# A one-step maximum over partitions, and another order of the first tile's statistics, weights and products in a fused LayerNorm, FFT and FFN kernel

## The chip, the cores and the metric

The kernel runs on one core of one Trainium2 chip. The metric is the device time of one execution in microseconds; lower is better. A run's time is a little longer than the span of its instructions in the profile.

## The reference

The kernel computes, for x of 8192 tokens by 448 features (f32), a layer norm, then two branches of it: a Fourier mixing branch (a transform over tokens and features, a small block-diagonal complex MLP with soft shrinkage on the spectrum, and back) and a GeGLU feed-forward branch. Their product is added to x.

```python
xn = _layernorm(x, axis=-1)
s = _A_ref(xn, A_w1, A_b1, A_w2, A_b2)
g = _silu(_B_ref(xn, B_w_gate, B_w_up, B_w_down))
return x + s * g
# _B_ref(x, w_gate, w_up, w_down) = (_gelu(x @ w_gate) * (x @ w_up)) @ w_down, F = 1792
```

The change touches neither the spectral branch's formulas nor the feed-forward's; it concerns how the first data and weights get ready.

## The kernel before, in words

The engines are TensorE (PE, with its weight loads as PEld), VectorE (DVE), ScalarE (ACT), GpSimd (POOL) and SyncE (SP), which issues the DMAs. Every operation is recorded through one helper, so almost every row of the profile has the same line (L180 before, L182 after); rows are told apart by the names of their tiles.

**Precision.** Products with f32 accuracy are made of f16 pieces: each operand is split into a high half (rounded to f16) and a low half (the remainder), and a product is the sum of high by high, high by low and low by high. Weights are first scaled by a power of two, which needs the largest magnitude of a weight block over all partitions and columns.

**Stages.** Tokens come in 16 chunks of 512 (four tiles of 128). Phase 1 normalises each chunk, makes the first step of the Fourier transform (`stage1`, tiles `m`, `ysb`, rows `bf<-xs,m`) and writes the pieces that the feed-forward needs to memory. The feed-forward (`ffn`) runs through the whole kernel: the first two chunks with 8 of the 14 weight tiles by plain products (`plain`, three terms), the others by a scheme with fewer products (`unit`, `product`) which needs combinations of the weights (`gu_comb`); the other 6 weight tiles follow in a second pass. Phase 2 does the spectral MLP, phase 3 the inverse transform (rows `bf<-u,mt`) and the final product; both are threaded between the feed-forward's matmuls on PE.

**The order of work.** A planner (`Pace`) runs while the kernel is built. Tasks are Python generators; each yields a time or an event, and the planner keeps a modelled time of each engine (`pace.free`), of each region of each tile, and of the last operation (`pace.last`). It records operations in the order of these modelled times; each engine then executes its operations in exactly that order. So a change of a cost in `Pace.cost` or of a due time (`T1`, `DT`, `END1`, `END2`, `END3`) reorders the programs of all engines. `Either` (`B`) sends an operation to DVE or POOL, whichever ends first by the model.

**The start.** `load_x` brings the first chunk's four tiles (in the order 0, 2, 1, 3), `gu_loads` the weight tiles `wst` of 704 KB each into four buffers. `begin` takes two tiles at a time (0 and 2, then 1 and 3): sums on DVE (`BN_STATS`, `BN_AGGR`), the power on POOL, a refinement on DVE (the root), the normalisation (`norm`, rows `x<-x,st`), and then per tile `token`: ACT casts to the high half `xs`, POOL or DVE subtracts for the low half, PE transposes both into a bank (`bf` or `bk<-ident,xs`), and a copy brings them to `xta`, tiles 0 and 2 by ACT, 1 and 3 by DVE. `gu_block` handles the weights of block b: DVE reduces the magnitudes over the columns (`fm<-wst`, then `fx<-fm`), `largest` takes the maximum over partitions, three small DVE steps make the scales (`fh`, `fc`, `fe`), and `gu_split` makes the high half on ACT and the low half on DVE or POOL (`wt`). For the first tile the halves are `ACTIVATE wt<-wst,fc` and `SCALAR_TENSOR_TENSOR wt<-wst,fc,wt`, each for up (4 slices) and gate (4 slices). `largest` works in two steps: an f32 matmul with the identity turns the columns of maxima into rows (`bf<-identf,fx`), DVE reduces along them (`mxr<-bf`), a second f32 matmul with the result repeated as weights brings it to all partitions (`bf<-identf,mxr`), and DVE copies it with a floor (`fx<-bf`).

`plain(0, 0)`, the first weight tile on the first chunk, works on two halves of 256 tokens; in each it goes through up and gate, and in each of these slice by slice: high by high, high by low, low by high. `down_weights(0)` loads the down-projection weights (`wo`, `xtb`, `cb<-in_down`), takes their maxima in eight DVE reductions (`dmx`) and splits them to `dw`; the down products (`bk<-dw,h`) come after both first chunks' `plain`.

Of the kernel before, what the change touches and what calls it, by code (L numbers as in the profile page):

```python
# [48 lines left out]
class Pace:  # L49
# [334 lines left out]
def afno_geglu_kernel(ctx, tc, x, gu, wd, mlp, b1, b2, c_m, c_mt, c_small, out):  # L384
# [32 lines left out]
    def part(bank_, *shape):  # L417
# [3 lines left out]
        return v.rearrange("p (a b) -> p a b", a=shape[1]) if len(shape) == 3 else v  # L421

    def pe():
        return pace.free.get("PE", 0.0) - 0.3
# [27 lines left out]

    def largest(dst, src, floor):

        w = src.shape[-1]
        b = yield from BF.get()
        T.matmul(b[0:w, 0:128], src, identf, start=True, stop=True)
        yield
# [86 lines left out]

    def norm(c, a):
        x4, st = EV["x4", c], EV["st", c]
        V.tensor_scalar(x4[:, a, :], x4[:, a, :], st[:, a, 6:7], st[:, a, 11:12],
                        op0=ALU.subtract, op1=ALU.mult)
# [103 lines left out]

    T1, DT = 84.0, 40.0

# [10 lines left out]
    def gu_block(b, to):  # L666

        f0, n = BLK[b]
        for i in range(n):
            yield ev("wl", f0 + i, 0)  # L670
            t = EV["wst", f0 + i, 0]
            V.tensor_reduce(fm[:, i, :, b], t[:, 0:8].rearrange("p (i k) f -> p i (k f)", i=2),
                            axis=AXIS.X, op=ALU.max, apply_absolute_value=True)
            yield
        mx = fx[:, :, b]
        if n == 2:
            V.tensor_tensor(mx, fm[:, 0, :, b], fm[:, 1, :, b], op=ALU.max)
        else:
            V.tensor_copy(mx, fm[:, 0, :, b])
        yield  # L680
# [6 lines left out]
        pow2(e, mxa)  # L687
        yield
        S.activation(fc[:, 4, b:b + 1], e[:, 1:2], AF.Copy, scale=2.0 ** -20)
        S.activation(fc[:, 5, b:b + 1], half[:, 1:2], AF.Copy, scale=2.0 ** (-25 - 2 * to))  # L690
        done("scales", b)
        for i in range(n):
# [4 lines left out]
            else:  # L697
                d, k = (yield from WO.get()), 2
            yield from gu_split(f, t, d, k)
            done("w", f)  # L700
            if to == 0:
# [20 lines left out]
    def gu_split(f, t, d, k):  # L722
# [443 lines left out]
    def plain(c, f):  # L1166

        yield ev("w", f)
        xT, h = EV["xT", c], EV["hT", c]
        g, u = (yield from BX.get()), (yield from BY.get())  # L1170
        w = wt[f]
        for q, tk in enumerate((slice(0, 256), slice(256, 512)) if (c, f) == (0, 0) else (slice(0, 512),)):
            if f == 0:
                for a in ((0, 2), (1, 3))[q] if c == 0 else range(CH):
                    yield ev("xp", c, a)
            for p, v in ((u, 0), (g, 4)):
                for t in range(3):
# [555 lines left out]

    END1, END2, END3 = T1 + NG * DT + 12.0, 1480.0, 1780.0

# [91 lines left out]
    def token(c, a, xs):  # L1827
# [31 lines left out]
    def begin():  # L1859
# [7 lines left out]

        def half(q):
            yield from stats(0, V, (q, q + 2))
            for a in (q, q + 2):  # L1870
                norm(0, a)
                tasks.append(pace.spawn(token(0, a, xss[a // 2]), pace.last))
                yield
# [8 lines left out]
        ST.put(EV["st", 0])  # L1882
        for q in range(2):
# [52 lines left out]
    def first():  # L1936
# [8 lines left out]
        tasks = []  # L1945
        yield 28.0
        done("phase", 1)
# [34 lines left out]
```

## Time and profile before

| | us |
|---|---|
| median of three runs | 1845.62 |
| lowest, highest | 1842.31, 1846.54 |
| the profiled execution | 1843.94 |
| its span, first to last instruction | 1842.2 |
| TensorE busy in the span | 1774.8 |
| VectorE, ScalarE, GpSimd busy | 1423.4, 1096.9, 582.9 |

In a timeline row stand the start, the duration, the engine, the line, the operation, `out<-in`, the shapes and a count (several like instructions are merged); in brackets the engine's idle time ahead of it and what ended that. The recorded duration of a PE row includes its latency, so the distance from one start to the next tells what it costs in a dense stretch. In a row of the stretches stand the length, and then for each engine the busy time and in parentheses the number of instructions. The mean granted TensorE clock of the profiled execution is 0.996.

### The profile page before, as it was taken

How to read it: one execution, taken by the hardware profiler on the slowest of the kernel's cores; microseconds unless marked ns; L12 is line 12 of the kernel's file. 1: busy time of each engine (PE TensorE's matmuls, PEld its weight loads, DVE VectorE, ACT ScalarE, POOL GpSimd, SP SyncE). 2: the span in 40 equal slices, each digit the busy share in tenths (PEclk: the TensorE clock that was granted, in tenths of full speed). 3: DMA queues.
4: the chain of work that ended last, by engine and by line, in shares of the span. 5: the costliest groups of instructions: out<-in, count | busy, mean ns of one | idle time of the engine just before them, and what ended most of it. 6: DMA issues, size and time to landing. Idle time of an engine off the chain costs nothing. (4 is left out here: it accounts for less than half of the span.)

```text
span 1842.2 us, 39141 instructions
## 1 busy us (share of the span) xinstructions
PE 1774.8 (96%) x15649; PEld 1423.5 (77%) x15649; DVE 1423.4 (77%) x2418; ACT 1096.9 (60%) x2105; POOL 582.9 (32%) x629
## 2 busy tenths in 40 slices
PE   6999999999999999999999999999999999999997
PEld 3447567666777777887877899989989898878886
DVE  7867788776866666656767788888888897888888
ACT  4746566655655555566766777677777774434443
POOL 3334444324523313100101233334432342333332
PEclk9999999999999999999999999999999999999999
DMA  7463665586564552132235544543344435999984
GB/s 263 140 168 113 195 193 177 164 233 186 147 165 115 150 155 82 44 92 74 64 114 166 147 104 117 117 104 88 98 103 117 112 97 156 327 297 319 289 311 148
DMA packets 345655, 287.79 MB, mean 156 GB/s; under 512 B 231840, under 2 KB 312736, under 8 KB 345472
## 3 DMA queue, kind: packets, MB, share of 16 engines
q1 hardware_dynamic: 345328, 285.26, 53.9%
q8 instruction: 122, 2.00, 0.4%
q14 instruction: 61, 0.50, 0.1%
q10 hardware_dynamic: 144, 0.03, 0.0%
HBM read 129.47 MB, written 106.61 MB: 128 GB/s over the span
## 5 line engine op out<-in xcount | busy, mean ns | idle before, releaser
L180 PEld LDWEIGHTS <-wt 128*128 128x128 f16 x9350 | 908.7, 98 | 191.6 <-issue 26.6
L180 PE MATMUL bk<-xta,wt 128*128 128x256 f16 (+1 forms) x5190 | 635.2, 276 | 9.2 <-DVE wt L180 4.6
L180 PE MATMUL bk<-xtb,wt 128*128 128x256 f16 x3120 | 382.2, 273 | 7.7 <-ACT v L180 7.7
L180 PE MATMUL bk<-dw,h 128*128 128x448 f16 (+1 forms) x2208 | 375.1, 321 | 9.0 <-DVE h L180 4.1
L180 PEld LDWEIGHTS <-h 128*128 128x128 f16 x2688 | 257.8, 98 | 140.8 <-DVE h L180 5.7
L180 ACT COPY v<-bk 128x512 f32<-128x512 f32 x208 | 121.7, 585 | 100.6 <-PE bk L180 99.3
L180 ACT COPY u<-bk 128x512 f32<-128x512 f32 x208 | 121.2, 585 | 70.9 <-PE bk L180 65.2
L180 POOL TENSOR_TENSOR wt<-wt 128x256 f32<-128x256 f32 x92 | 81.2, 883 | 185.9 <-DVE wt L180 174.4
L180 DVE TENSOR_TENSOR u<-bk,u 128x512 f32<-128x512 f32 x104 | 71.3, 686 | 86.4 <-PE bk L180 85.9
L180 POOL TENSOR_TENSOR zs<-t,zs 112x256 f16<-112x256 f32 (+2 forms) x41 | 35.5, 865 | 303.4 <-ACT zs L180 297.7
L180 ACT ACTIVATE u<-u,fc 128x512 f32<-128x512 f32 (+1 forms) x118 | 77.7, 669 | 62.0 <-DVE u L180 61.6
L180 PE MATMUL bk<-dw,wt 128*128 128x224 f16 (+1 forms) x864 | 103.1, 269 | 8.1 <-DVE pt L180 8.0
L180 POOL TENSOR_TENSOR v<-v,u 128x512 f32<-128x512 f32 x40 | 61.2, 1531 | 156.5 <-ACT v L180 152.5
L180 DVE SCALAR_TENSOR_TENSOR pt<-bk,fb,pt 128x448 f32<-128x448 f32 x112 | 74.7, 677 | 32.9 <-PE bk L180 32.0
L180 ACT CAST h<-wt 128x512 f16<-128x512 f32 (+1 forms) x128 | 68.6, 538 | 48.7 <-DVE wt L180 36.3
L180 ACT ACTIVATE th<-bk,fb 128x448 f32<-128x448 f32 x64 | 40.5, 633 | 85.4 <-PE bk L180 59.8
L180 PE MATMUL bf<-w2t,wn 112*128 112x112 f16 x1512 | 84.9, 213 | 0.0
L180 PEld LDWEIGHTS <-wn 112*128 112x128 f16 x1512 | 80.6, 98 | 2.4
L180 DVE TENSOR_TENSOR v<-bk,v 128x512 f32<-128x512 f32 x104 | 71.0, 683 | 12.9 <-PE bk L180 11.4
L180 POOL TENSOR_TENSOR h<-wt,h 128x512 f16<-128x512 f32 (+1 forms) x50 | 62.8, 1260 | 39.7 <-ACT h L180 37.8
L180 PEld LDWEIGHTS <-w1t 112*112 112x112 f16 x612 | 68.1, 130 | 7.5 <-issue 2.9
L180 DVE TENSOR_SCALAR x<-x,st 128x448 f32<-128x448 f32 x72 | 56.0, 790 | 22.3 <-POOL st L180 22.1
(197 smaller groups left out, 2934.4 us busy)
## 6 DMA issues: line engine op xcount, KB each, us to landing
wst<-in_gu SPq DMA_DIRECT2D x22, 704.0 KB, 5.4
xts<-sx SPq DMA_DIRECT2D x32, 480.0 KB, 2.9
x<-in_x SPq DMA_DIRECT2D x17, 896.0 KB, 5.9
t<-ysb SPq DMA_DIRECT2D x64, 224.0 KB, 3.4
prt<-th SPq DMA_DIRECT2D x64, 224.0 KB, 2.6
pt<-prt SPq DMA_DIRECT2D x64, 224.0 KB, 4.4
u<-t SPq DMA_DIRECT2D x32, 448.0 KB, 5.6
y<-t SPq DMA_DIRECT2D x30, 448.0 KB, 3.5
```

The source lines that it names most:

```text
L180: return self.pace.issue(self.name, kind, out, ins, lambda: fn(out, *args, **kw))
```

## The change

**`largest` in one step** for up to four columns: for each column one f32 matmul takes the column, repeated 128 times, as weights and the identity as moving data, so that each partition of the bank gets all 128 values; one DVE reduction over 128 columns per value then gives the maximum on all partitions. The floor moves into the step ahead (`fx<-fm`, now a scalar_tensor_tensor or tensor_scalar). This holds for all eight weight blocks and for the four-column maximum of the spectral weights; the down weights' eight and six columns keep the two steps.

**The first tokens.** The sums of both pairs of tiles come first; then the first pair's root and normalisations, then the first weight tile's maximum over columns, then the second pair's root, then the maximum over partitions and the scales, then the second pair's normalisations. The identity's f32 copy is made by ACT instead of DVE. Which engine copies a transposed bank is chosen by the planner's free times, no longer by the tile's number.

**The first weight tile.** Its other maxima's tasks start only once it is split. `plain(0, 0)` starts when the high halves are there, and in each half of the tokens takes first high by high for up and gate, then the inputs' low part, then the low weights. The small factors on ACT come after the split.

**Down weights** are started after weight tile 4 instead of tile 1.

**Due times** and costs: `T1` 84 to 78, `END2` 1480 to 1472, `END3` 1780 to 1772, the second chunk's start 28 to 26; the modelled cost of a DVE copy from f16 is smaller.

In the order of DVE's program before, from the first normalisation on (`x_102` are the first chunk's tokens, `st` their statistics, `wst` the raw weights, `fm` and `fx` their maxima):

```order
L180 TENSOR_SCALAR x_102<-x_102,st 128x448
L180 TENSOR_REDUCE fm<-wst 128x2
L180 TENSOR_SCALAR x_102<-x_102,st 128x448
L180 COPY fx<-fm 128x2
L180 BN_STATS st<-x_102 128x6
L180 BN_AGGR st<-st 128x2
```

And after, from the end of the second pair's sums to the same place:

```order
L182 TENSOR_SCALAR st<-st 128x2
L182 TENSOR_TENSOR st<-st 128x2 x2
L182 TENSOR_SCALAR st<-st 128x2
L182 TENSOR_TENSOR st<-st 128x2
L182 TENSOR_SCALAR x_102<-x_102,st 128x448 x2
L182 TENSOR_REDUCE fm<-wst 128x2
L182 TENSOR_SCALAR fx<-fm 128x2
```

The second pair's `BN_STATS` stood behind the weights' maximum and now stand ahead of the first pair's root; both normalisations stand together ahead of the maximum.

Further on in DVE's program, before, around the low half of the first weight tile (`wt0_82`; `wst_130` and `wst_138` are raw weights of later tiles):

```order
L180 TENSOR_SCALAR x4_102<-x4_102,st_122 128x448
L180 TENSOR_REDUCE fm_76<-wst_130 128x2
L180 COPY fx_77<-fm_76 128x2
L180 SCALAR_TENSOR_TENSOR wt0_82<-wst_111,fc_75,wt0_82 128x512 x2
L180 TENSOR_SCALAR fc_75<-fh_74,fe_73 128x1
L180 TENSOR_REDUCE fm_76<-wst_138 128x2
```

And after (`wst_115` and `wst_143` are those of later tiles):

```order
L182 TENSOR_SCALAR x4_102<-x4_102,st_111 128x448 x2
L182 SCALAR_TENSOR_TENSOR wt0_82<-wst_113,fc_75,wt0_82 128x512 x2
L182 TENSOR_SCALAR fc_75<-fh_74,fe_73 128x1
L182 TENSOR_REDUCE fm_76<-wst_115 128x2
L182 TENSOR_SCALAR fx_77<-fm_76 128x2
L182 TENSOR_REDUCE fm_76<-wst_143 128x2
```

The reductions of later tiles (two of them stood ahead of the low half) now all stand behind it.

On PE, before, the first f32 matmul of the maximum stands between the transposes of the first tile's high and low halves:

```order
L180 LDWEIGHTS xs_108
L180 MATMUL bf_142<-ident_72,xs_108 64x128
L180 MATMUL bf_156<-identf_96,fx_77 2x128
L180 LDWEIGHTS xs_108
L180 MATMUL bf_142<-ident_72,xs_108 128x128
```

And after, from the program's start:

```order
L2055 UNCONDITIONAL_BRANCH
L182 MATMUL bf_150<-identf_96,fx_77 128x128 x2
L182 LDWEIGHTS xs_108
L182 MATMUL bf_158<-ident_72,xs_108 128x128
L182 LDWEIGHTS xs_108
```

The two f32 matmuls now stand ahead of every transpose.

The diff, cut to its core:

```diff
+        if op == "tensor_copy" and ins[0].dtype == F16:
+            return 0.12 + 0.00056 * n
...
-    def largest(dst, src, floor):
+    def largest(dst, src, floor, between=None):
         w = src.shape[-1]
         b = yield from BF.get()
+        if w <= 4:
+            for i in range(w):
+                T.matmul(b[:, 128 * i:128 * i + 128], src[:, i:i + 1].to_broadcast([128, 128]), identf,
+                         start=True, stop=True)
...
+            V.tensor_reduce(dst, b[:, 0:128 * w].rearrange("p (i k) -> p i k", i=w), axis=AXIS.X, op=ALU.max)
+            BF.put(b)
+            return
...
-    T1, DT = 84.0, 40.0
+    T1, DT = 78.0, 40.0
...
+            if b == 0:
+                yield ev("first")
+                yield dve()
             V.tensor_reduce(fm[:, i, :, b], t[:, 0:8].rearrange("p (i k) f -> p i (k f)", i=2),
...
-        yield from largest(mxa, mx, 2.0 ** -30)
+        yield from largest(mxa, mx, 2.0 ** -30, None if b else (ev("reduced"), ev("root")))
...
+        if f == 0:
+            pace.then(lambda: done("w hi", 0))
...
-        yield ev("w", f)
+        yield ev("w hi", 0) if (c, f) == (0, 0) else ev("w", f)
...
+            if (c, f) == (0, 0):
+                for s, xs_ in ((0, 0), (0, 4), (1, 0)):
+                    if s:
+                        yield ev("w", 0)
+                    for p, v in ((u, 0), (g, 4)):
+                        for t in range(3 if xs_ else 4):
+                            T.matmul(p[:, tk], w[:, s, v + t], xT[xs_ + t][:, tk],
...
+                        yield pe()
+                continue
...
-    END1, END2, END3 = T1 + NG * DT + 12.0, 1480.0, 1780.0
+    END1, END2, END3 = T1 + NG * DT + 12.0, 1472.0, 1772.0
...
-            if a in (0, 2):
+            if max(pace.free["ACT"], pace.last) + 0.3 < max(pace.free["DVE"], pace.last):
                 S.copy(dst, src)
             else:
                 V.tensor_copy(dst, src)
...
-        V.tensor_copy(identf, ident)
-        yield from half(0)
-        yield from half(1)
+        S.copy(identf, ident)
+        yield from sums(0)
+        yield from sums(1)
+        for q in range(2):
+            if q:
+                yield ev("reduced")
+            root(q)
+            if q:
+                done("root")
+                yield ev("scaled")
+            for k, a in enumerate((q, q + 2)):
+                norm(0, a, sts[q][:, k])
+                tasks.append(pace.spawn(token(0, a, xss[a // 2]), dve()))
+            if not q:
+                done("first")
...
-        for b in range(PB[0][1]):
+        pace.spawn(gu_block(0, 0))
+        yield ev("w", 0)
+        for b in range(1, PB[0][1]):
             pace.spawn(gu_block(b, 0))
         combs = pace.spawn(gu_combs(near))
-        yield ev("w", 1)
+        yield ev("w", 4)
         yield pace.spawn(down_weights(0))
...
-        yield 28.0
+        yield 26.0
```

More of the change, by code (lines that the diff above doesn't have):

```diff
@@ L699, in gu_block @@
             yield from gu_split(f, t, d, k)
+            if not b:
+                factors_of()
             done("w", f)
@@ L1866, in begin, with sums, root @@
             xss.append((yield from XS.get()))
[L1868 to L1873, printed above, removed]
-        yield ev("xl", 0, 2)
-        V.tensor_copy(identf, ident)
-        yield from half(0)
-        yield from half(1)
+        x4 = EV["x4", 0]
+        sts = []
+        for _ in range(2):
+            sts.append((yield from ST.get()))
+        def sums(q):
+            s6, mv, rs = (sts[q][:, 0:2, c0:c1] for c0, c1 in ((0, 6), (6, 8), (8, 12)))
+            for k in range(2):
+                yield ev("xl", 0, q + 2 * k)
+                V.bn_stats(s6[:, k, :], x4[:, q + 2 * k, :])
+                V.bn_aggr(mv[:, k, :], s6[:, k, :])
+            V.tensor_scalar(rs[:, :, 0], mv[:, :, 1], EPS, None, op0=ALU.add)
+            G.tensor_tensor(rs[:, :, 1], rs[:, :, 0], mhalf[:, 0:2], op=ALU.pow)
+        def root(q):
+            v, y, t, r = (sts[q][:, 0:2, 8 + i] for i in range(4))
+            V.tensor_mul(t, y, y)
+            V.tensor_mul(t, t, v)
+            V.tensor_scalar(t, t, -128.0, 384.0, op0=ALU.mult, op1=ALU.add)
+            V.tensor_mul(r, t, y)
+        yield ev("xl", 0, 2)
+        S.copy(identf, ident)
[13 more added lines that the diff above has]
+                done("first")
         for e in tasks:
@@ L1881, in begin @@
         X4.put(EV["x4", 0])
-        ST.put(EV["st", 0])
+        for st in sts:
+            ST.put(st)
         for q in range(2):
```

42 lines of the change are left out of this document (31 added, 11 removed).

## The prediction

> **What bounds the kernel now.** I read the page's shares of busy time first, then the stretches, then TensorE's own timeline, and last the timeline of all engines over the first 20 us.
>
> ```profile
> span 1842.2 us, 39141 instructions
> ...
> PE 1774.8 (96%) x15649; PEld 1423.5 (77%) x15649; DVE 1423.4 (77%) x2418; ACT 1096.9 (60%) x2105; POOL 582.9 (32%) x629
> ```
>
> TensorE (PE) is busy for 1774.8 of 1842.2 us and its matmuls run in program order, so this change can gain only by closing some of the other 67 us. Two stretches show it (length, then busy us and count of PE, PEld, DVE, ACT, POOL, then clock, DMA share, GB/s).
>
> ```profile
> 40.00:50.00 10.00, 8.56 (x52) 4.31 (x52) 9.97 (x21) 4.77 (x11) 5.27 (x5) 1.00 0.55 213
> ...
> 100.00:150.00 50.00, 49.99 (x255) 24.83 (x254) 29.42 (x56) 21.55 (x36) 10.74 (x18) 1.00 0.72 204
> ```
>
> From 100 to 150 us PE has no gap: what is won ahead of that arrives there whole. TensorE's timeline has the gaps in brackets, with what ended them:
>
> ```profile
> 15.10 0.61 PE L180 MATMUL bk<-xta,wt 128*128 128x256 f16 x2 [1.80 <-ACT wt L180]
> 18.82 0.40 PE L180 MATMUL bk<-xta,wt 128*128 128x256 f16 x1 [3.11 <-DVE wt L180]
> ...
> 21.52 0.77 PE L180 MATMUL bf<-ident,xs 128*128 128x128 f16 x4
> 22.23 0.51 PE L180 MATMUL bk<-ident,xs 128*128 128x128 f16 x4
> ...
> 25.83 0.38 PE L180 MATMUL bf<-identf,fx 128*2 128x128 f32 x2
> 26.15 1.70 PE L180 MATMUL bk<-xta,wt 128*128 128x256 f16 x14
> 27.78 0.38 PE L180 MATMUL bf<-identf,mxr 2*128 2x2 f32 x2
> 28.09 0.50 PE L180 MATMUL bk<-xta,wt 128*128 128x256 f16 x3
> ...
> 29.00 2.32 PE L180 MATMUL bk<-xta,wt 128*128 128x256 f16 x11
> ...
> 39.44 0.52 PE L180 MATMUL bk<-ident,xs 128*128 128x128 f16 x4 [0.51 <-ACT xs L180]
> 40.96 0.38 PE L180 MATMUL bf<-identf,fx 128*2 128x128 f32 x2 [1.01 <-DVE fx L180]
> ...
> 49.79 0.52 PE L180 MATMUL bk<-ident,xs 128*128 128x128 f16 x4 [0.48 <-ACT xs L180]
> ...
> 53.63 0.38 PE L180 MATMUL bf<-identf,fx 128*2 128x128 f32 x2 [1.23 <-DVE fx L180]
> ...
> 60.68 0.38 PE L180 MATMUL bf<-identf,mxr 8*128 8x8 f32 x2 [0.41 <-DVE mxr L180]
> ...
> 116.25 15.49 PE L180 MATMUL bk<-dw,h 128*128 128x448 f16 x81
> ```
>
> PE runs without a break from 18.82 to 39 us; before that it waited 3.11 us for VectorE (DVE) to make the low half of the first tile's weights. From 39 to 61 us the five bracketed gaps sum to 0.51 + 1.01 + 0.48 + 1.23 + 0.41 = 3.64 us, while DVE is busy 9.97 of 10 us.
>
> **The start, step by step.** The durations come from the first 20 us of all engines:
>
> ```profile
> 0.72 1.84 SPq L180 DMA_DIRECT2D x<-in_x  x4
> ...
> 6.19 0.36 DVE L180 TENSOR_TENSOR st<-st 128x2 f32<-128x2 f32 x2 [0.91 <-POOL st L180]
> ...
> 6.99 0.51 DVE L180 TENSOR_SCALAR x<-x,st 128x448 f32<-128x448 f32 x1
> ...
> 8.38 1.22 DVE L180 TENSOR_REDUCE fm<-wst 128x2 f32<-128x1024 f32 x1 [0.88 <-DMA wst<-in_gu]
> ...
> 10.01 0.62 DVE L180 BATCH_NORM_STATS2 st<-x 128x6 f32<-128x448 f32 x1
> ...
> 10.16 0.59 PE L180 MATMUL bf<-identf,fx 128*2 128x128 f32 x2 [1.25 <-DVE fx L180]
> ...
> 10.68 0.75 PE L180 MATMUL bf<-ident,xs 128*128 128x128 f16 x4
> ...
> 11.36 0.75 PE L180 MATMUL bk<-ident,xs 128*128 128x128 f16 x4
> ...
> 11.46 0.91 ACT L180 COPY xta<-bf 128x896 f16<-128x896 f16 x1 [0.84 <-PE bf L180]
> ...
> 11.68 0.27 DVE L180 TENSOR_REDUCE mxr<-bf 2x1 f32<-2x128 f32 x1
> ...
> 11.88 0.60 DVE L180 TENSOR_TENSOR xs<-x,xs 128x448 f16<-128x448 f32 x1
> ...
> 12.04 0.58 PE L180 MATMUL bf<-identf,mxr 2*128 2x2 f32 x2
> ...
> 13.05 0.17 DVE L180 TENSOR_SCALAR fc<-fh 128x2 f32<-128x2 f32 x1
> ...
> 14.34 1.32 ACT L180 ACTIVATE wt<-wst,fc 128x512 f16<-128x512 f32 x2
> ...
> 17.16 2.26 DVE L180 SCALAR_TENSOR_TENSOR wt<-wst,fc,wt 128x512 f16<-128x512 f32 x2
> ```
>
> The fourth input tile lands 4.5 us after its issue, as the DMA view gives it:
>
> ```profile
> x<-in_x SPq DMA_DIRECT2D x1, 224.0 KB, 4.5
> ```
>
> Four issues take 1.84 us, so the fourth goes out at 0.72 + 3 x 0.46 = 2.1 us and lands at 6.6. Both pairs' sums now stand in one stretch, and the second pair's are done one tile's sums (0.62) and two small steps later, about 7.6 us. Only then come the first pair's root (6.19 to 6.99, so 0.80), to 8.4; its two normalisations (0.51 each), to 9.45; the weights' maximum (1.22), to 10.65; and its small step (0.17), to 10.85. The first normalisation comes 1.4 us later than now, at 8.4 against 6.99, and PE's first f32 matmul 0.7 us later than 10.16. That is what the change costs.
>
> The maximum over partitions now is two f32 matmuls and one DVE reduction. Each matmul has 128 columns of weights and 128 moving; the trace has only f32 matmuls with one side narrow, 0.59 us (2 columns of weights) and 0.58 us (2 moving). Two of the new kind cost 1.2 us if the wide loads hide beside a matmul, 2.4 if they don't. I take 1.4, near the first end, because with the f16 products loads and matmuls overlap (14 in 1.63 us from 26.15): 10.85 to 12.25. DVE has the second pair's root (0.80) and a subtraction (0.60) until 12.25 anyway, which covers it; at 2.4 the cover is gone and all below comes 1.0 later. The reduction reads 256 columns; between 0.27 (128) and 1.22 (1024) the line gives 0.41, so the factors stand at about 13.1, as now (13.05 + 0.17).
>
> What is queued behind this wait: all 16 transposes of the first pair stand after the two f32 matmuls on PE, and ScalarE's (ACT) copies wait for them. Four take 0.68 us (10.68 to 11.36): the low halves end at 14.25 and 14.95, ACT's copies (0.91 each) at 15.2 and 16.1, and the two weight splits (0.66 each) at 16.75 and 17.4. PE begins the tile at 16.75 instead of 15.10, but no longer stops in it: eight products of high weights, six of the inputs' low parts and eight transposes lie ahead of the first low weight, by the rates above over 2.5 us, and DVE, with the other maxima now behind, makes the low weights from 16.75 on (2.26 us for both now). So PE is dense from 16.75 instead of 18.82. It has two more products to do (0.4), and one new gap: ACT copies the second pair's transposes, 0.91 each, right ahead of the second half's products, about 1.0 us. The second weight tile began at 29.2 (29.00 and two products); now 29.2 - 2.07 + 0.4 + 1.0 = 28.5: **0.7 us gained**, or 0.3 lost if the first f32 pair takes 2.4.
>
> **The gaps from 39 to 61 us.** The second chunk's transposes (0.51, 0.48) now stand behind one more whole weight tile on PE, over 4 us of products. The maxima's results (1.01, 1.23) waited for a DVE that had the down weights' eight reductions in between; those and their loads come after tile 4's weights now. I take 3.3 of the 3.64 us as closed, with 0 and 3.64 as bounds, since the rows name the two causes and the order removes both. The down weights cost nothing by being later: their first use is at 116.25. On SyncE's queue the third chunk's input stands behind one more weight load that waits for its buffer, some 10 us; its first reader is far off:
>
> ```profile
> L180 DVE BATCH_NORM_STATS2 st<-x x5: 614/619/623, 80.7 to 119.3; 128x6 f32<-128x448 f32 x5
> ```
>
> **The f32 matmuls on a full PE.** Once PE is dense, the old two steps take 0.32 + 0.31 = 0.63 us (25.83 to 26.15, 27.78 to 28.09). Two new matmuls take 0.62 to 1.24, and I take 0.7, by the same near end. Four blocks in the start and three later: 7 x 0.07 = 0.5 us lost (0 to 4.3). The four-column maximum of the spectral weights, four matmuls, loses 4 x 0.35 - 0.63 = 0.8 (0.6 to 1.9). Between 140 and 700 us PE also waited for the step that is dropped:
>
> ```profile
> PE bf L180 <- DVE mxr L180: 1.2, 1, 1.2
> ```
>
> That 1.2 us goes. [...]
>
> **Sum.** -0.7 - 3.3 + 0.5 + 0.8 - 1.2 = -3.9 us. The profiled execution took 1843.94 (span 1842.2 and 1.74 around it) and would take 1840.0; the median of the runs, 1845.62, lies 1.7 above it and becomes 1841.7. That is 0.21% less; 0.2% (3.7 us) is about what a measurement of this kernel can tell from no change.
>
> **Rivals.** *Given back* (0.22): DVE is the bound there, an earlier PE only waits longer, and the gaps stay. For it: 9.97 of 10 us busy. Against: eight reductions leave the stretch. With the gaps kept, -0.7 + 0.5 + 0.8 - 1.2 = -0.6: 1845.0.
>
> *The last stage is pushed to the end* (0.12), the slower case. The due times of the later stages move by 8 us, but their place in PE's program moves otherwise: the last stage's first matmul has 102 more FFN matmuls ahead of it, and its last stands 49 rows from the end of the program, not 157.
>
> ```profile
> L180 PE MATMUL bf<-u,mt x192: 349/352/362, 1558.4 to 1822.5; 128*128 128x448 f16 x192
> ```
> ```profile
> 1560.00:1580.00 20.00, 20.00 (x175) 16.86 (x173) 17.25 (x27) 10.44 (x20) 5.79 (x6) 1.00 1.00 323
> ...
> 1820.00:1840.00 20.00, 10.97 (x102) 9.52 (x100) 15.66 (x26) 4.50 (x8) 1.34 (x2) 0.95 0.16 58
> ```
>
> At 2026 FFN matmuls over these 264 us, 0.13 each, the stage starts 13 us later in PE's work and ends 7 later (54 matmuls): the same transfers, at a DMA share of 1.0, get 6 us less. If the transfers bind, the last tile comes 6 + 7 - 4 = 9 us later, at 1831.5, and DVE's closing work, 15.66 us in the last 20, slides by 9 minus what it now idles there, 4.3: about +5, 1850.3. It decides once that tile lands later than 1827. Against it: the share falls to 0.16 at the end.
>
> *A warm array* (0.14): four transposes take 0.71 us from 21.52 and 0.51 from 22.23, so PE speeds up about 3 us after it became dense at 18.82. The burst of f32 matmuls and transposes now lasts from 10.85 to 14.95, longer than any before 18.82, and ends 1.8 us ahead of the products; if the speed holds over the pause, the 3.4 us of slow work (18.82 to 22.23) shrink by 0.51/0.71 to 2.4, and the sum is -4.9: 1840.7. [...]
>
> *The forecast* (0.52): -2.5 to -6 us, two thirds of it beyond 3.7. That the change does what it says is not in doubt: the order shows the maxima and the low weights in their new places.
>
> **Chances.** Faster by over 0.2%: 0.35 of the forecast and 0.14 of the warm array, 0.49. Slower by over 0.2%: 0.10 of the slower rival's 0.12. Within 0.2%: the rest, 0.17 + 0.22 + 0.02 = 0.41. The range runs from 1836.5 (the warm array with nothing lost to f32, -6.2, 1839.4, less what the median of three runs of one kernel can differ) to 1847.5, part of the way to the slower rival; about a tenth is left out at each end.
>
> **What would show it.** Right: PE dense from 16 to 18 us on, the second weight tile at 28 to 29, no bracket over 0.5 us from 39 to 61, the first product with dw at 111.5 to 113 instead of 116.25. Wrong: f32 pairs of over 1 us on a dense PE, the first weight product after 17.8, gaps of 1 us left between 30 and 61, dw after 115, or the last mt matmul within 8 us of PE's end with DVE's closing work after it.

## The result, and the profile after

The changed kernel takes 1827.51 us (median; 1826.53 to 1832.07), the kernel before beside it 1844.35 (1842.31 to 1846.54): a ratio of 0.9913 with a 95% interval of 0.9900 to 0.9927. That is 16.8 us less, where 3.9 were forecast, and below the range, whose low end was 1836.5. The profiled execution took 1828.43.

The page after, in the rows that answer to those quoted of before:

```profile
span 1826.6 us, 39098 instructions
...
PE 1769.9 (97%) x15653; PEld 1425.8 (78%) x15653; DVE 1413.2 (77%) x2400; ACT 1101.2 (60%) x2103; POOL 585.6 (32%) x640
```

The span fell by 15.6 us. TensorE's idle time, span less busy, fell from 67.4 to 56.7, its busy time by another 4.9. TensorE's timeline of the first part (bracket: idle ahead of the row, and what ended it):

```profile
10.76 1.19 PE L182 MATMUL bf<-identf,fx 128*128 128x128 f32 x4 [10.76 <-DVE st L182]
11.75 0.77 PE L182 MATMUL bf<-ident,xs 128*128 128x128 f16 x4
...
16.31 2.53 PE L182 MATMUL bk<-xta,wt 128*128 128x256 f16 x11 [1.74 <-ACT wt L182]
...
19.95 0.77 PE L182 MATMUL bk<-ident,xs 128*128 128x128 f16 x4
20.65 1.03 PE L182 MATMUL bk<-xta,wt 128*128 128x256 f16 x4
...
22.56 0.61 PE L182 MATMUL bf<-identf,fx 128*128 128x128 f32 x4
23.01 0.50 PE L182 MATMUL bk<-ident,xs 128*128 128x128 f16 x4
24.51 0.60 PE L182 MATMUL bk<-xta,wt 128*128 128x256 f16 x4 [0.99 <-ACT xta L182]
...
28.49 0.59 PE L182 MATMUL bk<-xta,wt 128*128 128x512 f16 x2
...
46.68 0.68 PE L182 MATMUL bf<-identf,fx 128*128 128x128 f32 x4 [0.66 <-DVE fx L182]
...
112.65 7.54 PE L182 MATMUL bk<-dw,h 128*128 128x448 f16 x39
```

All of this is nearly as forecast: dense from 16.31, the one new gap 0.99, the second weight tile at 28.49, one gap of 0.66 left between 39 and 61 us (the forecast allowed 0.5), and the first product with `dw` at 112.65 instead of 116.25.

To see where the rest came from, the start times of the same piece of work are compared. The feed-forward's matmuls (those that write `bk`, transposes left out) are counted through the trace; there are 12,038 of them in every trace here, and "product n" is the n-th from zero. Tile for tile they stand in the same order in all twenty traces, but for 44 products between 154 and 219 in the kernel before with all new due times, so product n is the same work in each.

| product | 600 | 700 | 1100 | 3500 | 12037 (last) |
|---|---|---|---|---|---|
| before, us | 158.5 | 169.5 | 235.4 | 584.1 | 1833.8 |
| after, us | 154.9 | 166.4 | 223.9 | 570.9 | 1818.4 |
| difference | -3.6 | -3.0 | -11.4 | -13.1 | -15.4 |

The start's gain arrives at 155 us. Then 8 us come between products 700 and 1100, where the change edits little: two chunks' due times and one weight block's maximum. Two stretches there, first of before, then of after (length; busy us and count of PE, PEld, DVE, ACT, POOL; clock, DMA share, GB/s):

```profile
176.00:184.00 8.00, 6.93 (x58) 5.37 (x56) 8.00 (x10) 6.04 (x11) 7.84 (x10) 1.00 0.11 41
184.00:194.00 10.00, 7.31 (x37) 4.70 (x38) 8.19 (x10) 5.15 (x12) 4.44 (x3) 0.66 0.36 97
```
```profile
176.00:184.00 8.00, 8.00 (x73) 6.95 (x72) 7.65 (x9) 5.93 (x11) 7.26 (x8) 1.00 0.01 2
184.00:194.00 10.00, 9.46 (x60) 5.62 (x59) 10.00 (x15) 6.63 (x13) 6.07 (x9) 1.00 0.79 195
```

Before, TensorE issued 95 matmuls in these 18 us, after 133: it was idle for 3.76 us, and the granted clock of 0.66 over 10 us means 6.8 us at half speed. TensorE's and VectorE's timelines of before there:

```profile
184.81 0.61 PE L180 MATMUL bk<-xta,wt 128*128 128x256 f16 x4 [1.48 <-DVE wt L180]
187.31 1.30 PE L180 MATMUL bf<-xs,m 128*128 128x448 f16 x3 [1.89 <-DVE ysb L180]
```
```profile
175.97 1.61 DVE L180 TENSOR_TENSOR xs<-x,xs 128x896 f16<-128x896 f32 x1
...
183.13 1.62 DVE L180 SCALAR_TENSOR_TENSOR wt<-cb,fc,wt 128x1024 f16<-128x1024 f32 x1
184.67 2.04 DVE L180 TENSOR_TENSOR xs<-x,xs 128x896 f16<-128x896 f32 x1
186.64 0.61 DVE L180 SCALAR_TENSOR_TENSOR ysb<-bf,ysb 128x448 f16<-128x448 f32 x1
```

`wt<-cb` is the low half of the last of eight combined weight tiles; `xs<-x,xs` are the two low halves of a token chunk, the one with the due time `T1 + 2 * DT` (164 before, 158 after; "the 164 chunk" below). VectorE, busy without a break, does the weight between the two, and TensorE waits for it, and then for `ysb` behind the second. After, on VectorE and on TensorE:

```profile
174.22 1.28 DVE L182 SCALAR_TENSOR_TENSOR wt<-cb,fc,wt 128x1024 f16<-128x1024 f32 x1 [0.67 <-ACT wt L182]
...
180.47 1.62 DVE L182 TENSOR_TENSOR xs<-x,xs 128x896 f16<-128x896 f32 x1
...
187.22 1.07 DVE L182 TENSOR_TENSOR xs<-x,xs 128x896 f16<-128x896 f32 x1
```
```profile
188.89 0.74 PE L182 MATMUL bf<-xs,m 128*128 128x448 f16 x3 [0.54 <-DVE ysb L182]
```

The combined weight now comes 9 us earlier, ahead of both low halves; the waits of 1.48 and 1.89 us have become one of 0.54, and no half clock follows (the next is at 377 us).

### The profile page after: what moved, and what is told of

It is laid out like the page before. It is cut to its first block, busy times and chain, and to the rows that moved or that the text cites. A ratio compares the mean times of both kernels' runs of the same rounds, so it can differ in the third digit from the quotient of the medians.

```text
span 1826.6 us, 39098 instructions
## 1 busy us (share of the span) xinstructions
PE 1769.9 (97%) x15653; PEld 1425.8 (78%) x15653; DVE 1413.2 (77%) x2400; ACT 1101.2 (60%) x2103; POOL 585.6 (32%) x640
## 5 line engine op out<-in xcount | busy, mean ns | idle before, releaser
L182 DVE TENSOR_TENSOR u<-bk,u 128x512 f32<-128x512 f32 x104 | 71.5, 687 | 77.6 <-PE bk L182 77.4
L182 ACT ACTIVATE u<-u,fc 128x512 f32<-128x512 f32 (+1 forms) x118 | 77.5, 669 | 52.0 <-DVE u L182 51.8
L182 POOL TENSOR_TENSOR v<-v,u 128x512 f32<-128x512 f32 x31 | 44.6, 1440 | 125.8 <-ACT v L182 122.7
L182 POOL TENSOR_TENSOR h<-wt,h 128x512 f16<-128x512 f32 (+1 forms) x57 | 69.2, 1217 | 30.8 <-ACT h L182 30.6
L182 DVE SCALAR_TENSOR_TENSOR gl<-v,fc,gl 128x512 f32<-128x512 f32 (+1 forms) x70 | 47.2, 691 | 37.5 <-ACT gl L182 37.4
```

What stands on the lines that cost most here:

```text
L182: return self.pace.issue(self.name, kind, out, ins, lambda: fn(out, *args, **kw))
```

## Experiments: undoing one part

The first theory (D) was that the due times made this order. Its rivals were the one-step maximum in the later blocks (M), the later down weights (W), and a plain reshuffling of the plan (C). Each kernel puts in or takes out one of them.

**The due times alone**, in the kernel before:

```diff
-    T1, DT = 84.0, 40.0
+    T1, DT = 78.0, 40.0
...
-    END1, END2, END3 = T1 + NG * DT + 12.0, 1480.0, 1780.0
+    END1, END2, END3 = T1 + NG * DT + 12.0, 1472.0, 1772.0
...
-        yield 28.0
+        yield 26.0
```

> The kernel before with only the due times of the change: chunks from 78 instead of 84, the third stage's ends 8 earlier, begin1 at 26 instead of 28. Theory D (the due times): the chunks' preparation meets the weights' combinations at another place, and that alone removes the stalls and the half clock at 180-200 us; the time is about 11 us below the kernel before (1833), with no slice of half clock near 190 us. Theory M (the one-step maximum in the later blocks) and theory W (down weights later): within 2 us of the kernel before (1842 to 1846), with the half clock near 190 us still there. Theory C (no part by itself: any shift of the plan lands the work of VectorE elsewhere): 3 to 10 us either way, at places that need not be 180-200 us.

**The old due times** in the changed kernel (the same diff, reversed):

> The changed kernel with the three old due times (84, 1480 and 1780, 28). Theory D: only the start's 4 us are left, 1839 to 1841, with stalls again at 180-200 us. Theories M and W: 1827 to 1830, as the changed kernel. Theory C: anywhere from 1828 to 1842.

**The one-step maximum for the first block only**, in the changed kernel:

```diff
-        if w <= 4:
+        if w <= 4 and between:
```

> The changed kernel with the one-step maximum for the first weight block alone; the other blocks and the spectral maximum take the old two steps. Theory M: the gap of 3.6 us at 39-61 us comes back, and the 11 us beyond the start with it, 1839 to 1842. Theory D and W: only the 39-61 us gaps come back, 1828 to 1832. Theory C: 1828 to 1842.

**The down weights early again**, in the changed kernel:

```diff
-        yield ev("w", 4)
+        yield ev("w", 1)
```

> The changed kernel with the down weights started after the second weight (as before) and not after the fifth. Theory W: the VectorE and ScalarE work of the down weights falls again between the weights' combinations, the loss is the 11 us beyond the start, 1838 to 1840. Theories D and M: within 2 us of the changed kernel, 1826 to 1830. Theory C: 1828 to 1842.

Measured, each kernel beside the kernel before, which took 1844.35 to 1846.27 in all these comparisons (the interval is that of the ratio; idle is span less TensorE's busy time, all in us):

| kernel | us | ratio to before, 95% | idle | product 1100 | product 3500 | last |
|---|---|---|---|---|---|---|
| before | 1844.35 | | 67.4 | 235.4 | 584.1 | 1833.8 |
| before, new due times | 1855.39 | 1.0033 to 1.0070 | 75.0 | 235.3 | 581.6 | 1849.7 |
| changed | 1827.51 | 0.9900 to 0.9927 | 56.7 | 223.9 | 570.9 | 1818.4 |
| changed, old due times | 1857.07 | 1.0043 to 1.0077 | 73.6 | 223.2 | 578.8 | 1846.8 |
| changed, two-step maximum | 1848.63 | 1.0003 to 1.0026 | 70.5 | 226.2 | 581.3 | 1837.5 |
| changed, down weights early | 1850.20 | 1.0014 to 1.0037 | 70.4 | 223.0 | 574.7 | 1840.0 |

None of D, M and W holds. Any one undoing costs the whole gain and more (21 to 30 us), though the three concern different things. At product 1100, however, the picture is plain: all three undoings still have their lead of 9 to 12 us there, and the new due times alone have none. So the 8 us around 180 us belong to none of the three parts, and the undoings lose theirs later, by other waits. For the later program that is nearest to theory C, though all three lie above its range, which ended at 1842; for the 180 us it is something not yet named.

## Experiments: how far one plan is from its neighbours

The same kernel once more, and due times moved by half a microsecond, so that only the order differs.

> The changed kernel itself, once more, beside the kernel before on another chip: both theories 1826 to 1832, so that the losses of the four undoings are those of their plans and not of the chip. If the gain belonged to the chip, 1840 or more.

```diff
-    T1, DT = 78.0, 40.0
+    T1, DT = 77.5, 40.0
```

> The changed kernel with the chunks due half a microsecond earlier (77.5 for 78): no instruction is added, removed or changed, only the order. Theory P (the place of the chunks' preparation, good within a microsecond or more): 1825 to 1831, and no more than 40 us of idle time on TensorE. Theory S (scatter: the change is worth its start, some 4 us, and every plan draws its own idle time and half-clock windows on top): anywhere from 1830 to 1850, with idle time and half-clock windows at places that the changed kernel does not have, after 600 us too.

The same with 78.5:

> The changed kernel with the chunks due half a microsecond later (78.5 for 78), order alone. Theory P: 1825 to 1831. Theory S: anywhere from 1830 to 1850, and not the same as with 77.5.

And the kernel before, with 83.5 for 84:

> The kernel before with the chunks due half a microsecond earlier (83.5 for 84), order alone. Theory P: 1842 to 1848, with the stall and the half clock near 190 us still there. Theory S: anywhere from 1840 to 1862, above the kernel before as likely as the changed kernel's nudges are above it, and with other stalls.

| kernel | us | ratio to before, 95% | idle | product 1100 | product 3500 | last |
|---|---|---|---|---|---|---|
| changed, again | 1831.30 | 0.9904 to 0.9933 | 56.8 | 223.3 | 573.1 | 1821.2 |
| changed, 77.5 | 1834.00 | 0.9921 to 0.9947 | 62.0 | 222.4 | 569.5 | 1820.7 |
| changed, 78.5 | 1836.14 | 0.9928 to 0.9961 | 63.8 | 226.4 | 581.5 | 1826.8 |
| before, 83.5 | 1844.23 | 0.9979 to 1.0000 | 65.2 | 239.1 | 580.7 | 1835.4 |

The gain is not the chip's: on another chip the changed kernel took 1831.30. Half a microsecond of a due time costs 3 to 5 us in the changed kernel and nothing in the kernel before. Neither theory (P, the place holds within a microsecond; S, scatter) was right whole: the gain is no single lucky plan (three plans have 10 to 15 us of it), but the 78.5 run loses 6 of the 11 us by which it leads at product 1000 before product 1500 (212 to 287 us), by waits of its own.

Next, the ends of the later stages by themselves, and larger steps of `T1`:

```diff
-    END1, END2, END3 = T1 + NG * DT + 12.0, 1472.0, 1772.0
+    END1, END2, END3 = T1 + NG * DT + 12.0, 1480.0, 1780.0
```

> The changed kernel with the old ends of the later stages (1480 and 1780 for 1472 and 1772), the chunks due at 78 as in the change; nothing before the second stage differs. Theory E (the run with all three old due times lost its 18 us after 1000 us to the ends): as the changed kernel up to 900 us, then a loss of 10 to 18 us, 1840 to 1848. Theory T (it lost them to the chunks' due times): 1828 to 1834.

The reverse in the kernel before:

> The kernel before with the new ends (1472 and 1772) alone. Theory E: the loss of 10 to 18 us that the kernel before with all new due times showed after 1000 us is here, 1853 to 1860. Theory T: 1843 to 1849.

`T1` 80 in the changed kernel:

> The changed kernel with the chunks due at 80 for 78, order alone. Theory T (the chunks' due times have a best value, with a loss on both sides that grows with the distance: 3 us at 77.5, 5 us at 78.5): 1837 to 1845. Theory E: 1828 to 1836. Theory S (each plan draws its own stalls): either.

`T1` 82 in the kernel before:

> The kernel before with the chunks due at 82 for 84, order alone. Theory T: 1847 to 1853, between the kernel before (1846) and the kernel with all new due times (1855). Theory S: anywhere from 1836 to 1860. Nothing below 1836 if the change has a worth of its own of 10 us that no due time of the kernel before gives.

| kernel | us | ratio to before, 95% | idle | product 1100 | product 3500 | last |
|---|---|---|---|---|---|---|
| changed, old ends | 1839.32 | 0.9958 to 0.9982 | 67.2 | 224.7 | 571.5 | 1829.3 |
| before, new ends | 1843.76 | 0.9988 to 1.0005 | 66.9 | 235.1 | 585.2 | 1835.1 |
| changed, 80 | 1843.27 | 0.9980 to 0.9997 | 68.4 | 225.8 | 577.6 | 1830.2 |
| before, 82 | 1842.98 | 0.9981 to 1.0006 | 65.7 | 234.4 | 579.8 | 1834.5 |

The old ends cost the changed kernel some 8 to 12 us (by its two medians), all but 1 us of it behind 1100 us and most of it from 1500 to 1630; the new ends give the kernel before nothing. So theory E holds, in place and nearly in size (1839.32 for 1840 to 1848), for the changed kernel and not for the kernel before. Theory T's best due time agrees with the run at 80 (1843.27) and not with the run at 82 (1842.98, where it asked for 1847 to 1853). The kernel before stands at 1843 to 1846 in four plans and at 1855 with all new due times: moving due times down gives it no lead.

## Experiments: the order at 180 us, and who keeps the lead

In all five plans of the old code so far the last combined weight is written at 183 to 190 us, behind a low half of the 164 chunk; in all plans of the changed code at 172 to 177, ahead of both. What is left of the change to do that is the start, or the modelled cost of copies. The start alone, without the three parts undone above (and with the old cost of copies):

> The start of the change alone (first tokens' statistics in one stretch, first block's one-step maximum and low weights, the other blocks after it), with the old due times, the old maximum in the later blocks, the down weights after the second weight and the old cost of copies. Theory K (the start's lead moves the last combined weight of the second load ahead of the preparation of the chunk due at 164, which takes away the stall and the half clock at 184-193 us): product 1100 of the FFN starts at 223 to 227 us (old code 234 to 239), the last combined weight is written at 172 to 178, no half clock between 180 and 195; the time 1832 to 1842 by what the later plan loses. Rival O (another part does it): product 1100 at 230 us or later, the last combined weight behind 183, time 1839 to 1846.

And the order itself, flipped in the kernel before by 4 us on one due time:

```diff
-            yield T1 + (c - PL) * DT
+            yield T1 + (c - PL) * DT + (4.0 if c == PL + 2 else 0.0)
```

> The kernel before with one due time changed: the chunk due at 164 at 168, so that the last combined weight is planned before both of that chunk's low parts and not between them. Theory K: the waits of 1.5 and 1.9 us and the half clock near 186 us go; product 1100 starts 4 to 7 us earlier than in the kernel before (228 to 232), time 1837 to 1842. Rival O: TensorE waits for that chunk's later preparation instead, product 1100 within 2 us of the kernel before, time 1842 to 1848.

The same line with `- (4.0 ...)` in the changed kernel:

> The changed kernel with the same one due time moved the other way: the chunk due at 158 at 154, so that the last combined weight is planned between that chunk's two low parts, as in the kernel before. Theory K: a wait of 1 to 3 us for the weight or the chunk's low parts near 180 us and a half-clock window behind it, product 1100 starts 4 to 7 us later (228 to 231), time 1832 to 1838. Rival O: product 1100 within 2 us of the changed kernel, time 1827 to 1833.

| kernel | us | ratio to before, 95% | idle | product 700 | product 900 | product 1100 | product 3500 | last |
|---|---|---|---|---|---|---|---|---|
| before | 1844.35 | | 67.4 | 169.5 | 202.3 | 235.4 | 584.1 | 1833.8 |
| before, chunk at 168 | 1854.90 | 1.0044 to 1.0070 | 71.2 | 170.8 | 197.3 | 237.7 | 588.1 | 1843.5 |
| changed | 1827.51 | 0.9900 to 0.9927 | 56.7 | 166.4 | 193.1 | 223.9 | 570.9 | 1818.4 |
| changed, chunk at 154 | 1855.39 | 1.0050 to 1.0079 | 77.4 | 165.9 | 195.7 | 230.9 | 582.2 | 1845.1 |
| start alone | 1850.00 | 1.0018 to 1.0042 | 68.3 | 169.9 | 196.5 | 226.9 | 573.9 | 1839.1 |

*Flipped in the changed kernel*, VectorE has the old order and TensorE the old wait:

```profile
175.28 1.61 DVE L182 TENSOR_TENSOR xs<-x,xs 128x896 f16<-128x896 f32 x1
...
181.14 1.32 DVE L182 SCALAR_TENSOR_TENSOR wt<-cb,fc,wt 128x1024 f16<-128x1024 f32 x1
...
183.75 1.64 DVE L182 TENSOR_TENSOR xs<-x,xs 128x896 f16<-128x896 f32 x1
```
```profile
182.52 0.61 PE L182 MATMUL bk<-xta,wt 128*128 128x256 f16 x4 [2.29 <-DVE wt L182]
...
205.30 0.87 PE L182 MATMUL bf<-identf,fx 128*128 128x128 f32 x4 [3.42 <-DVE fx L182]
```

From product 700 to 1100 it takes 65.0 us, as before (65.9), where the changed kernel takes 57.5. So one due time that restores this order takes back 7.5 of the 8.4 us. Theory K is shown in this direction by product 1100 (230.9, within its 228 to 231); only 2.29 of the 7 us lost there are the weight's own wait, and the rest is mostly a longer wait for a later weight block's maximum (3.42; 0.94 in the changed kernel) with a half-clock window behind it (a clock of 0.83 over the 10 us from 204 us, so 3.4 us at half speed). The time of 1855.39 lies 17 us above K's range: some 20 us more go behind product 1100, which K does not explain.

*Flipped in the kernel before*, the stall and the half clock at 184 us do go (a clock of 1.00 from 184 to 194 us, where it was 0.66), and product 900 comes 5.0 us earlier. But the lead is gone again by product 1000. TensorE's row, and ScalarE's, of that place:

```profile
222.44 2.72 PE L180 MATMUL bk<-xta,wt 128*128 128x256 f16 x12 [7.23 <-ACT u L180]
```
```profile
214.89 0.63 ACT L180 ACTIVATE th<-bk,fb 128x448 f32<-128x448 f32 x1 [7.66 <-DMA prt<-th]
...
221.28 0.63 ACT L180 ACTIVATE th<-bk,fb 128x448 f32<-128x448 f32 x1 [3.74 <-DMA prt<-th]
```

ScalarE waits 7.66 and 3.74 us for a buffer `th` that a store still reads, and the copies that TensorE needs stand behind that in its queue (the first `u` at 221.81 us). So neither theory's numbers came: the same flip that gave 5 us met a transfer that was not done, and product 1100 came 2.3 us later than in the kernel before, the end 10 us later.

*The start alone* has the new order (weight written at 177.66, low halves at 183.92 and 190.67), 57.0 us from product 700 to 1100, and no half clock at the old place (twelve products from 187.48 us take 1.47 us, as at full speed); theory K's signs came (226.9 at product 1100), its time of 1832 to 1842 did not. The new order does not need a lead on TensorE: at product 700 this kernel stands at 169.9 us, the kernel before at 169.5. Over all twenty traces the stretch from product 700 to 1100 takes 62.3 to 66.8 us with the old start and 56.7 to 60.3 with the new one, but for the 65.0 of the changed kernel flipped. No run separates the parts of the start. The lead at product 700 is missing here for a reason that answers to the forecast: with the old maximum and the early down weights together (and the old due times and cost of copies), the gaps at 39 to 61 us are back as one of 2.66 us, with a clock of 0.89 over 15 us behind and around it, so 3.3 us at half speed:

```profile
50.67 0.51 PE L180 MATMUL bk<-ident,xs 128*128 128x128 f16 x4 [2.66 <-ACT xs L180]
```
```profile
45.00:60.00 15.00, 12.34 (x67) 5.78 (x65) 11.61 (x34) 10.47 (x24) 7.83 (x7) 0.89 0.48 154
```

Either of the two parts alone is enough to close them: with only one of them undone, TensorE's longest gap from 30 to 61 us is 0.22.

The start alone leads by 10 us at product 3500 and is still slower at the end: 11 us go between 1040 and 1430 us, and 5 more behind that. One run below moves the ends; the other two try to improve the changed kernel, whose longest wait behind the start is 3.39 us for `dmx`, at 374 us, with a half-clock window behind it (a clock of 0.66 over the 5 us from 376 us).

> The start alone with the new ends of the later stages (1472 and 1772), everything else as in the run of the start alone. Theory T (the ends have to follow the lead): the 10 to 12 us of lead at 700 us are still there at the last FFN product, and the time is 1831 to 1837. Theory S (each plan draws its own idle time in the later stages): the lead at 700 us is the same 10 to 12 us, and the time is anywhere from 1836 to 1852.

```diff
+        if p:
+            yield pace.now + 5.0
         yield from largest(dm, dmx[:, fs], 2.0 ** -30)
```

> The changed kernel with the second half's down maximum put 5 us later in the plan (27 FFN products ahead of its transpose on TensorE), which takes away the changed kernel's longest wait, 3.4 us for dmx at 374 us, and the half-clock window behind it. If a stall costs its length and the half clock that follows: 3.4 and 1.7 us less, 1823 to 1828. If the rest of the plan eats it (scatter): 1828 to 1836.

The same, with the ends at 1468 and 1768:

> The changed kernel with the down maximum 5 us later in the plan, and the ends 4 earlier again (1468 and 1768). Theory T: the 5 us gained before 600 us are kept, 1822 to 1828. Theory S: 1828 to 1840.

| kernel | us | ratio to before, 95% | idle | product 1100 | product 3500 | product 9000 | last |
|---|---|---|---|---|---|---|---|
| start alone | 1850.00 | 1.0018 to 1.0042 | 68.3 | 226.9 | 573.9 | 1429.8 | 1839.1 |
| start alone, new ends | 1833.65 | 0.9923 to 0.9949 | 57.3 | 227.7 | 574.8 | 1417.5 | 1822.9 |
| changed, later dmx | 1832.03 | 0.9920 to 0.9948 | 59.2 | 223.0 | 564.8 | 1410.8 | 1819.7 |
| changed, later dmx, ends 4 earlier | 1825.70 | 0.9878 to 0.9910 | 52.9 | 223.0 | 567.5 | 1410.7 | 1815.6 |

With the new ends the start alone keeps its lead: 16.4 us for two numbers that act behind 700 us. TensorE's waits from 1050 to 1500 us, with the old ends and then with the new:

```profile
PE bf L180 <- DVE k L180: 6.0, 6, 2.0
PE bk L180 <- DVE pt L180: 4.5, 7, 1.0
```
```profile
PE bf L180 <- DVE k L180: 2.8, 3, 1.2
PE bk L180 <- DVE pt L180: 1.1, 5, 0.2
```

The second stage's results (`k`) and the second pass's partial sums (`pt`) come late for TensorE in the one plan and not in the other. Moving `dmx` took its wait away but put one of 2.34 us for `mxr` in its place, and the time (1832.03) fell into the range for a plan that eats the gain:

```profile
382.77 0.38 PE L182 MATMUL bf<-identf,mxr 6*128 6x6 f32 x2 [2.34 <-DVE mxr L182]
```

The 6 us that it led at product 3500 were lost behind 1470 us; with the ends moved on by 4, the kernel takes 1825.70, the lowest here. That is 20 us below the kernel before, but only 1.8 to 5.6 below the changed one's two medians, which lie 3.8 apart.

The ends are no rule, though. The changed kernel with the early down weights led by 9.4 us at product 3500, had the new ends, and still lost 15.6 by the last product, all of it behind 1040 us; the kernel before lost nothing with the new ends. So theory T of the last runs holds for these two codes and not as a rule. Why one plan of the later stages has 10 us more of waits than another stays open.

## Why the prediction was right in its parts and wrong in its sum

- **The start, -0.7: right, in part by luck.** Forecast dense from 16.75, a gap of 1.0, second weight tile at 28.5; measured 16.31, 0.99, 28.49. The first f32 pair, taken as 1.4 us, took 0.99 (10.76 to 11.75), so the tile began 0.44 us early. From there to the second weight tile it took 12.18 us where the forecast has 11.75; the clock rose 5.6 us after the first product, where before it had risen 3.4 us after PE became dense. The two misses cancel.
- **The gaps from 39 to 61 us, -3.3 of 3.64: right.** 0.66 is left, and `dw` began 3.6 us earlier, within the forecast's 111.5 to 113. The forecast counted on two causes going; with either of the change's two parts back alone, the gaps stayed closed.
- **The f32 matmuls on a dense array, +0.5: wrong sign.** Two of the new kind take 0.45 us (22.56 to 23.01), less than the old two steps' 0.63; the seven blocks' pairs take 0.44 to 0.52, together 1.15 us less than seven times 0.63. Each f32 matmul is two rows 0.11 to 0.13 us apart, wide or narrow; in the old steps another 0.2 us passed from the last f32 row to the next product, twice, and the forecast's price of a narrow matmul had that in it. What sets the 0.45 is not shown.
- **The spectral maximum, +0.8: right sign, too large.** Its four matmuls take 0.96 us for the old 0.63, so +0.33.
- **The wait for `mxr`, -1.2: not won.** The row is gone, but the same maximum of the spectral weights now waits as long ahead of its only step (`mst` are its columns):

```profile
PE bf L182 <- DVE mst L182: 1.2, 1, 1.2
```

- **The step that failed is what the sum put at nothing.** For all work behind 116 us it has three terms, some +0.2 + 0.8 - 1.2 = -0.2 us, and takes the rest over from the profile of before without a reason. The order rows had been read at the start only. The runs showed 8.4 us there from product 700 to 1100, and 4.0 more by the last product. In the main they go with an order: on a busy VectorE the last combined weight now stands ahead of the 164 chunk's low halves. The new start alone makes this order, and one due time that flips it in the changed kernel takes back 7.5 of the 8.4. Flipped in the kernel before, it won 5.0 us by product 900, which the wait for a transfer took away. How the start moves the weight in the planner's times was not traced.
- **The rest is this plan's luck.** The later stages took 10 us and more in other plans with about the same lead at product 1100, and nothing here; no run shows why.
- **"This change can gain only by closing some of the other 67 us" was wrong too.** Of 15.6 us of span, 4.9 came out of the busy time: matmuls at half clock count as busy (from 445.5 to 448.8 us in the kernel before, at a clock of 0.50, TensorE was busy for all 3.30 us). Between the start and the last 20 us, before had 10.2 us at half clock (6.8 near 186 us, 3.4 near 445) and after 3.4 (near 377); the 6.8 fewer, at half speed, are 3.4 of the 4.9.
- **The rivals.** *Given back* did not come: DVE's share from 40 to 50 us was the reason to fear it, and the gaps closed. *The last stage is pushed to the end* showed its sign and not its cost: the last `mt` matmul begins 3.8 us ahead of TensorE's end (11.5 before), but at 1814.8 us, ahead of the 1827 that was to decide, and from TensorE's end to the span's it takes 8.0 us for 8.1 before. *A warm array* fell: four transposes from 19.95 to 20.65 us still took 0.70 us, and the clock rose at 21.9 us, 5.6 us after the first product.

## What to carry to other kernels

Where a planner sets the order, a change of a few microseconds edits the whole program: compare the orders up to the end, above all on the engine that has no slack, and look for pairs of tasks that nearly tie. Give the forecast a range as wide as the plan's own scatter: 19 kernels with the same work took from 1826 to 1857 us, and 4 us on one due time moved one of them by 24 to 28. What this plan of the later stages gives can go with the next edit. Read a saturated engine's busy time together with its clock, and refit the due times of the later stages after a gain ahead of them, by measurement.

## What the runs showed of the hardware

- **Inside the program the half clock came in stretches of 3.4 us or a multiple** (6.83 and 3.41 us in the kernel before, 3.41 in the changed one), and the same wait brought one in one run and none in another. The granted clock is 1.0 or 0.5 in all twenty traces, with nothing between. The changed kernel ran twice with the same program; the first row of each pair is TensorE's after a wait of 2.1 us, the second the stretch. First run, then second:

```profile
348.00 1.47 PE L182 MATMUL bk<-xta,wt 128*128 128x256 f16 x12 [2.11 <-ACT v L182]
...
348.00:353.00 5.00, 5.00 (x42) 4.10 (x42) 5.00 (x7) 4.65 (x9) 4.87 (x5) 1.00 0.53 164
```
```profile
348.03 2.19 PE L182 MATMUL bk<-xta,wt 128*128 128x256 f16 x12 [2.12 <-ACT v L182]
...
348.00:353.00 5.00, 4.97 (x29) 3.46 (x29) 5.00 (x7) 4.65 (x8) 4.86 (x5) 0.66 0.53 164
```

  Twelve products take 1.47 or 2.19 us. In each trace all changes of the clock lie on one grid of 3.413 us (within 0.004 us in those of before and after), at another place in each run. By this grid the first run's wait fell into two windows, and the one that holds most of it was idle for 53% (1.80 us); the second run's fell into one, idle for 62% (2.12 us). Over all twenty traces, from the first rise to 30 us before the end, 56 full-speed windows were followed by a half-speed one: 54 were idle for 55.7% or more, two for 51%. Of the 10338 that were followed by another full-speed window none was idle for more than 55.1%. In the traces of before and after alone these are three windows, idle for 62, 72 and 81%, against 1034, none of them idle for more than 53%. So in these counts, but for the two at 51%, the idle share of one window tells the two kinds apart. Two short waits made up such a share in the kernel before, those of 1.48 and 1.89 us (62% of the window that ends at 186.0 us).
- **The first rise of the clock came late in one run.** With the kernel before at 83.5, whose program is the same there, eight products from 24.70 us took 1.89 us, and 1.05 in the kernel before; the clock rose at 30.6 us instead of 22.2. Its first product came 1.8 us later than in the kernel before (the first f32 matmul waited 2.98 us for `fx`, and 1.25 in the kernel before), product 100 4.8 us later with the same waits between, so the clock cost 3.0. The column of the granted clock shows 1.00 ahead of its first entry, so this is seen in the rows only:

```profile
24.70 1.89 PE L180 MATMUL bk<-xta,wt 128*128 128x256 f16 x8
```
```profile
22.67 1.05 PE L180 MATMUL bk<-xta,wt 128*128 128x256 f16 x8
```

  In the 14 traces with the new start it rose between 19.9 and 23.4 us, in the six with the old one between 22.2 and 30.6, and product 100 came at 41.7 to 44.0 us and at 44.6 to 51.5. So the profile of before that the prediction used had the earliest rise of the six, and in most of these traces the dense start is worth more than its 4 us there. Why the clock rose so late in one is open: in the two windows ahead of its last one TensorE was already idle for only 7% and 0%. Nor did a burst of f32 matmuls and transposes raise it: in the changed kernel TensorE was busy for all 3.50 us from 11.0 to 14.5 us, and eleven products from 16.31 us still took 2.53 us (1.36 in the kernel before from 24.54 us, behind the rise).
